# Hashed attention and a squared-ReLU layer on one core: scores and values in 64x64 array tiles taken in turn, hash and totals in 64x32 tiles

## The chip, the cores and the metric

The kernel runs on one core of one Trainium2 chip. The metric is the device time of one execution in microseconds (us). Three runs of the kernel before gave 877.64, 877.53 and 878.19 us; their median is 877.64.

## The reference

Attention over 4 batches of 8 heads, 768 tokens and 64 features, in which a query sees only the keys of its own hash bucket; its output goes through a layer with squared ReLU.

```python
q_bits = np.einsum('bhsd,dk->bhsk', q, proj) > 0        # 6 bits
k_bits = np.einsum('bhsd,dk->bhsk', k, proj) > 0
mask = q_bucket[:, :, :, None] == k_bucket[:, :, None, :]
scores = where(mask, q @ k.T / 8, -1e9)
attn = exp(scores - max); attn = attn / (attn.sum(-1) + 1e-9)
x = (attn @ v) as (4 * 768, 512)
h = np.maximum(x @ w_in, 0)                             # w_in 512 x 2048
out = (h * h) @ w_out                                   # w_out 2048 x 512
```

The weights arrive as 64-bit floats and are rounded to 32 bits on the chip.

## The kernel before

The program has two stages. The first does attention, 16 pairs of heads one after the other; the second, from L717 on, does the layer by a scheme with seven products for eight, and the change leaves its code as it was but for the name of one PSUM pool.

**A pair of heads.** Features stand on the partitions, head 0 on 0 to 63 and head 1 on 64 to 127. `load_pair` (L279) brings q and k through eight DMAs on SP's queue, `features` (L330) turns each by one VectorE transpose. `hash_bits` (L337) multiplies with the projection, in tiles of the array with 64 rows and 32 columns, all eight at once; `signs` (L351) makes bits of it by eight ScalarE operations of 32 partitions, and `weigh` (L379) scales the key bits by one more. Bits are padded into two tiles `bits` on the partitions of the heads.

**Scores.** There are six blocks of 128 keys, `kt`. `score` (L386) makes scores with the keys on the partitions, for the queries 0 to 511 and then 512 to 767 (`CUTS`): for each cut a bf16 product of the bits and an fp32 product of the features into the same PSUM tile, head 0 in rows 0 to 63 of the array and head 1 in rows 64 to 127, with 128 columns each (tiles 64*128, two at once). A PSUM tile `turn` has two banks, one per head; the pool `ps_s` has three of them. ScalarE takes the exponent (L413) into one of four tiles `e`, the ring. An extra column of e holds a tiny constant for the keys that no query meets.

**Totals and values.** `add_up` (L419) adds the six e on VectorE. `attend` (L432) multiplies with the values, 128 keys in the rows and 64 columns per head (tiles 128*64, two at once), over all six blocks into `xo`. `sum_up` (L448) sums `total` over the keys with a matrix of ones (tiles 128*32, four at once), VectorE turns and inverts that, `spread` (L472) multiplies with a selection matrix, and `normalize` (L483) turns the result and multiplies it with xo into `x_t`, which a DMA stores.

**Weights beside it.** Each pair also rounds two pieces of 128x512 weights: `part_weight` (L136, two VectorE operations), `place_power` (L153, two ScalarE operations, L160 and L161), `round_weight` (L163, three VectorE operations). `sum_in` (L522) forms sums of w_in for the second stage.

**Order.** It is written out by hand (`manual_schedule`, the loop from L614); each engine takes its instructions in that order, and SP's DMAs are issued in it. TensorE's order in a pair is: scores of blocks 0 and 1; hash of the next pair; totals of the pair before; values of blocks 4 and 5 of the pair before; `spread`; scores 2 and 3; values 0 and 1; scores 4 and 5; values 2 and 3. `finish` (L579) does the middle of this. After the last pair come its totals, its values 4 and 5 and its `spread`, and right behind that the first product of the second stage (L717). VectorE's order at the end is the sums of blocks 4 and 5, `sum_x` for the second stage, the inversion, two more `sum_x`, `normalize`, and the last piece of weights.

Of the kernel before, what the change touches and what calls it, by code (L numbers as in the profile page):

```python
# [34 lines left out]
def kernel(  # L35
# [25 lines left out]
    CUTS = (0, 512), (512, S)  # L61
# [49 lines left out]
    NIN = 2 * NFT  # L111
    pieces = [
        (moe_w_in, i // 2 * P, i % 2 * HF + j * PIECE) for j in range(2) for i in range(NIN)
    ] + [(moe_w_out, i * P, 0) for i in range(NFF)]
    raws, parts, goals = {}, {}, {}
    ins = [p_t.tile([P, NFT, 2, PIECE], FP32, name=f"in{j}") for j in range(2)]

    def goal(i):
        if i < 2 * NIN:
            return ins[i // NIN][:, i % NIN // 2, i % 2]  # L120
        return p_t.tile([P, DM], FP32, name="out_piece", bufs=3)

    def load_weight(i):
        src, r, c = pieces[i]
        if src.dtype != U64:
            goals[i] = goal(i)
            nc.sync.dma_start(out=goals[i], in_=src[r:r + P, c:c + PIECE])
            return
        raw = p_w.tile([P, PIECE, 2], U32, name="raw", bufs=3)
        nc.sync.dma_start(  # L130
            out=raw.rearrange("p f w -> p (f w)"),
            in_=src.bitcast(U32)[r:r + P, 2 * c:2 * (c + PIECE)],
        )
        raws[i] = raw

    def part_weight(i):  # L136

        if i not in raws:
            return
        high = raws[i][:, :, 1]  # L140
        power = p_w.tile([P, PIECE], U32, name="power")
        top = p_w.tile([P, PIECE], U32, name="top")
        nc.vector.tensor_scalar(
            out=power, in0=high, scalar1=20, scalar2=0x7FF,
            op0=ALU.logical_shift_right, op1=ALU.bitwise_and,
        )
        nc.vector.tensor_scalar(
            out=top, in0=high, scalar1=0xFFFFF, scalar2=0x100000,
            op0=ALU.bitwise_and, op1=ALU.bitwise_or,
        )  # L150
        parts[i] = power, top

    def place_power(i):  # L153


        if i not in parts:
            return
        power = parts[i][0]
        small = p_w.tile([P, PIECE], U8, name="small")
        nc.scalar.activation(out=small, in_=power, func=ACTF.Relu, bias=excess)  # L160
        nc.scalar.activation(out=power, in_=small, func=ACTF.Copy, scale=2.0**23)  # L161

    def round_weight(i):  # L163

        raw = raws.pop(i, None)
        if raw is None:
            return keep_weight(i)
        goals[i] = goal(i)
        low, high = raw[:, :, 0], raw[:, :, 1]
        power, top = parts.pop(i)  # L170
        nc.vector.scalar_tensor_tensor(  # L171
            out=power, in0=high, scalar=0x80000000, in1=power,
            op0=ALU.bitwise_and, op1=ALU.bitwise_or,
        )
        one = top.bitcast(FP32)
        nc.vector.scalar_tensor_tensor(  # L176
            out=one, in0=low, scalar=2.0**-32, in1=top, op0=ALU.mult, op1=ALU.add,
# [7 lines left out]
    def keep_weight(i):  # L185

        t = goals.pop(i)
        j, c = divmod(i, NIN)
        if j >= 2:
            nc.sync.dma_start(out=w_out_1[:, i - 2 * NIN], in_=t)  # L190
        elif c == NIN - 1:
# [31 lines left out]
    picks = const.tile([P, P], FP32, name="picks")  # L223
    which = const.tile([P, 2, HS // 32], FP32, name="which")
    NRING = 4
    ring = [const.tile([P, 2, S + 1], FP32, name=f"e{i}") for i in range(NRING)]
# [4 lines left out]
    def constants():  # L231
# [4 lines left out]
        for h in range(2):  # L236
            r = h * D
            nc.vector.memset(gains[r:r + N + 1], -FAR / 2 * N)
            nc.vector.memset(gains[r:r + N], FAR / 2)
            nc.vector.memset(bases[r:r + N + 1], -FAR / 2 * N)  # L240
            nc.vector.memset(bases[r:r + N], -FAR / 2)
            nc.vector.memset(spans[r:r + N], FAR)
        for r in range(0, P, NR_B):
            nc.vector.memset(lifts[r:r + N + 1], 1.0)
            nc.vector.memset(lifts[r:r + N], -SMALL)
        for pair in all_bits:
# [3 lines left out]
        for e in ring:  # L250
            nc.vector.memset(e[:, :, S:S + 1], TINY)


        for g in range(4):
            cut = picks[:, g * 32:(g + 1) * 32]
            at = 64 * (g // 2)
            nc.gpsimd.tensor_tensor(
                out=cut, in0=ident[:, at:at + 32], in1=ident[:, at + 32:at + 64], op=ALU.add
# [8 lines left out]
    def load_first():  # L267

        for src, name in ((q, "q_nat"), (k, "k_nat")):
            t = p_qk.tile([P, SB, 2, D], FP32, name=name)  # L270
# [4 lines left out]
            nat[0, name] = t  # L275
# [3 lines left out]
    def load_pair(pr):  # L279
# [3 lines left out]
        for src, name in ((q, "q_nat"), (k, "k_nat")):  # L283
            t = p_qk.tile([P, S], FP32, name=name)
            for g in range(4):
                h, e = divmod(g, 2)
                nc.sync.dma_start(  # L287
                    out=t[g * 32:(g + 1) * 32].rearrange("i (c d) -> i c d", d=32),
                    in_=src[b, 2 * j + h].rearrange("(c i) (e d) -> e i c d", i=32, e=2)[e],
                )  # L290
            nat[pr, name] = t
# [10 lines left out]
    def first_features(w, r):  # L302

        if r == 0:
            feat[0, w] = p_f.tile([P, S], FP32, name=f"feat{w}")
        tp = turn("tp")[:, 0]
        for i in range(SB // 2):
# [3 lines left out]
                in_=nat[0, ("q_nat", "k_nat")[w]][:, t].rearrange("p h d -> p (h d)"),  # L311
                identity=ident,
            )
        out = feat[0, w][:, r * HS:(r + 1) * HS]
# [6 lines left out]
    void = ps_o.tile([P, 1024], FP32, name="xo")  # L321

    def keep_busy(n, w=512):

        for _ in range(n):
            nc.tensor.matmul(  # L326
                out=void[:, 0:w], lhsT=busy[:, 0:P], rhs=busy[:, 0:w], start=True, stop=True
            )

    def features(pr, w):  # L330

        feat[pr, w] = p_f.tile([P, S], FP32, name=f"feat{w}")
        nc.vector.transpose(out=feat[pr, w], in_=nat[pr, ("q_nat", "k_nat")[w]])  # L333
# [3 lines left out]
    def hash_bits(pr, banks, ws=(0, 1), cs=(0, 1)):  # L337


        for w in ws:  # L340
            hashed[pr, w] = banks
            for c in cs:
                g = 2 * w + c
                for h in range(2):
# [3 lines left out]
                        rhs=feat[pr, w][rows, c * HS:(c + 1) * HS], start=True, stop=True,  # L348
                    )

    def signs(pr, w):  # L351
        bits[pr, w] = t = all_bits[pr % 2][w]
        for c in range(2):
            at = slice((2 * w + c) * NR_B, (2 * w + c + 1) * NR_B)
            for h in range(2):
                nc.scalar.activation(  # L356
                    out=t[h * D:h * D + NR_B, c * HS:(c + 1) * HS], in_=hashed[pr, w][at, h, 0:HS],
                    func=ACTF.Sign, scale=HUGE, bias=lifts[at],
                )

# [18 lines left out]
    def weigh(pr):  # L379

        t = bits[pr, 1]
        nc.scalar.activation(out=t, in_=t, func=ACTF.Copy, scale=gains)

    weights = {}

    def score(pr, kt):  # L386

        e = ring[len(weights) % NRING]
        weights[pr, kt] = e
        key = slice(kt * P, (kt + 1) * P)  # L390
        sts = []

        def products(st, lo, hi, src, first):
            for h in range(2):
                rows = slice(h * D, (h + 1) * D)
                nc.tensor.matmul(  # L396
                    out=st[:, h, 0:hi - lo], lhsT=src[pr, 1][rows, key],
                    rhs=src[pr, 0][rows, lo:hi], start=first, stop=not first,
                )


        if (pr, kt) == (0, 0):
            for lo, hi in CUTS:
                sts.append(turn("st"))
                products(sts[-1], lo, hi, feat, True)
        for i, (lo, hi) in enumerate(CUTS):
            if len(sts) <= i:
                sts.append(turn("st"))
                products(sts[i], lo, hi, bits, True)
                products(sts[i], lo, hi, feat, False)  # L410
            else:
                products(sts[i], lo, hi, bits, False)
            nc.scalar.activation(  # L413
                out=e[:, :, lo:hi], in_=sts[i][:, :, 0:hi - lo], func=ACTF.Exp, scale=scale
            )

    totals, outs, recs = {}, {}, {}

    def add_up(pr, kt):  # L419

        if kt == 1:
            totals[pr] = p_n.tile([P, 2, S], FP32, name="total")
            nc.vector.scalar_tensor_tensor(
                out=totals[pr], in0=weights[pr, 0][:, :, 0:S], scalar=SB * TINY,
                in1=weights[pr, 1][:, :, 0:S], op0=ALU.add, op1=ALU.add,
            )
        else:
            nc.vector.tensor_tensor(  # L428
# [69 lines left out]

# [984 lines left out]
```

## Time and profile before

| | |
|---|---|
| median of three runs | 877.64 us |
| span of the profiled execution, first to last instruction | 875.8 us |
| attention, first scores to the first product L717 | 9.3 to 330.2 us |
| TensorE busy | 864.5 us (99%) |
| VectorE busy | 760.1 us (87%) |
| ScalarE busy | 391.7 us (45%) |
| GpSimd busy | 107.1 us (12%) |
| mean granted TensorE clock | 0.997 |

The profile gives no time of its own for the profiled execution beyond the span; the median stands 1.8 us above it. A row of instructions names the line, the engine (PE is TensorE, DVE is VectorE, ACT is ScalarE, POOL is GpSimd, SP issues DMAs), the operation, the tiles written and read, and the shape. Behind a TensorE row stands the tile of the array, rows by columns; an fp32 product shows as two passes, so "x4" is two products. A record of a product reaches until its last result has landed, so records of a stream overlap, and its pace is read from the starts.

### The profile page before, as it was taken

The page shows a single profiled execution, that of the slowest core. Times are in us where ns is not written, and L with a number is a line of the kernel's source. Part 1 is how long each engine was busy: PE and PEld are TensorE (multiplying, and loading weights), DVE is VectorE, ACT ScalarE, POOL GpSimd, SP SyncE. Part 2 cuts the span into 40 slices and gives each one's busy share as a digit, 9 for nine tenths or more (in the row PEclk, how much of TensorE's full clock was granted, in tenths as well). Part 3 has the DMA queues.
Part 4 walks back from the last instruction along what each step waited for, and adds up shares of the span by engine and source line. Part 5 has one row for each costly group of instructions (what it writes and reads, how often), then busy time and mean ns, then how long its engine had stood idle before and what let it go on. Part 6 is the DMA issues. An engine that isn't in the chain of part 4 may idle for free.

```text
span 875.8 us, 12135 instructions
## 1 busy us (share of the span) xinstructions
PE 864.5 (99%) x4340; PEld 519.3 (59%) x4340; DVE 760.1 (87%) x1099; ACT 391.7 (45%) x673; POOL 107.1 (12%) x172
## 2 busy tenths in 40 slices
PE   8999999999999999999999999999999999999996
PEld 4444444444444444444688865556888755568885
DVE  5999999999999998888689978888889788888875
ACT  6988788888888852222211123332111233321110
POOL 2000000000000001554032111112000211110002
PEclk9999999999999999999999999999999999999998
DMA  9787967999879526999787874536756754355565
GB/s 176 146 154 134 232 156 150 194 244 234 179 172 226 164 98 223 294 263 288 299 291 259 219 172 156 173 125 219 282 161 177 166 169 152 124 169 158 154 171 109
DMA packets 224131, 167.09 MB, mean 191 GB/s; under 512 B 164448, under 2 KB 181344, under 8 KB 224064
## 3 DMA queue, kind: packets, MB, share of 16 engines
q1 hardware_dynamic: 189152, 87.19, 41.7%
q0 software_dynamic: 12528, 41.30, 15.2%
q10 hardware_dynamic: 22384, 37.76, 14.3%
q8 instruction: 36, 0.59, 0.3%
q14 instruction: 31, 0.25, 0.1%
HBM read 124.52 MB, written 41.68 MB: 190 GB/s over the span
## 4 chain that ended last, share of the span: by engine, by line
PE 95%; DVE 2%; SPq 1%; DMA 1%; issue 0%; ACT 0%; DVEq 0%
PE acc L717 40%; PE st L396 17%; PE acc L936 16%; PE xo L438 13%; PE acc L889 6%; PE hash L346 1%; PE tot L455 1%; DVE total L428 1%; DMA q_nat<-in_q_dram 1%; SPq L287 1%; PE xo L326 0%; PE tp L309 0%; DVE power L171 0%; DVE top L176 0%; DVE feat L333 0%
## 5 line engine op out<-in xcount | busy, mean ns | idle before, releaser
L413 ACT ACTIVATE e<-st 128x1024 f32<-128x1024 f32 x192 | 144.9, 810 | 44.4 <-PE st L396 40.7
L396 PE MATMUL st<-feat,feat 64*128 64x512 f32 (+1 forms) x768 | 150.4, 483 | 0.0
L438 PE MATMUL xo<-e,v_nat 128*64 128x512 f32 (+1 forms) x768 | 134.8, 492 | 0.0
L717 PE MATMUL acc<-b,leaf 128*128 128x256 f32 x600 | 133.1, 379 | 0.0
L717 PEld LDWEIGHTS acc<-b,leaf 128*128 128x128 f32 x600 | 113.8, 190 | 16.2 <-issue 0.9
L428 DVE TENSOR_TENSOR total<-total,e 128x1536 f32<-128x1536 f32 x64 | 112.4, 1756 | 8.1 <-ACT e L413 3.6
L438 PEld LDWEIGHTS xo<-e,v_nat 128*64 128x64 f32 x768 | 51.3, 136 | 82.2 <-issue 74.0
L936 PE MATMUL acc<-t_x,w_unit 128*128 128x512 f32 x192 | 90.2, 592 | 0.0
L396 PEld LDWEIGHTS st<-feat,feat 64*128 64x128 f32 x768 | 66.0, 188 | 32.4 <-issue 22.6
L717 PE MATMUL acc<-t,leaf 128*128 128x256 f32 x336 | 76.2, 380 | 0.0
L356 ACT ACTIVATE bits<-hash,lifts 32x384 bf16<-32x384 f32 x120 | 68.7, 573 | 1.9
L717 PEld LDWEIGHTS acc<-t,leaf 128*128 128x128 f32 x336 | 63.7, 190 | 9.1 <-DVE t L516 0.5
L801 DVE SCALAR_TENSOR_TENSOR b<-h 128x512 f32<-128x512 f32 x96 | 65.7, 692 | 3.0
L396 PE MATMUL st<-bits,bits 64*128 64x256 bf16 (+1 forms) x384 | 63.0, 325 | 0.7 <-ACT bits L356 0.5
L936 PE MATMUL acc<-x,w_unit 128*128 128x512 f32 x128 | 60.1, 592 | 0.0
L717 PE MATMUL acc<-x,w_unit 128*128 128x512 f32 x128 | 56.5, 593 | 0.0
L717 PE MATMUL acc<-b_t,leaf 128*128 128x256 f32 x240 | 53.8, 379 | 0.0
L936 PEld LDWEIGHTS acc<-t_x,w_unit 128*128 128x128 f32 x192 | 36.5, 190 | 28.8 <-issue 26.8
L724 ACT COPY two<-acc 128x256 f32<-128x256 f32 (+1 forms) x29 | 12.5, 432 | 87.7 <-PE acc L717 69.1
L724 ACT COPY one<-acc 128x256 f32<-128x256 f32 (+1 forms) x29 | 12.5, 432 | 84.3 <-PE acc L717 55.5
L717 PEld LDWEIGHTS acc<-b_t,leaf 128*128 128x128 f32 x240 | 45.5, 190 | 6.2
L396 PEld LDWEIGHTS <-bits 64*128 64x128 bf16 x384 | 23.6, 93 | 41.9 <-issue 37.7
(159 smaller groups left out, 1166.5 us busy)
## 6 DMA issues: line engine op xcount, KB each, us to landing
leaf<-w_out ACTq DMA_DIRECT2D x142, 256.0 KB, 3.2
w_unit<-w_in SPq DMA_DIRECT2D x16, 640.0 KB, 4.0
raw<-in_moe_w_in_dram SPq DMA_DIRECT2D x16, 512.0 KB, 5.5
raw<-in_moe_w_out_dram SPq DMA_DIRECT2D x16, 512.0 KB, 4.5
w_unit<-w_in SPq DMA_DIRECT2D x8, 896.0 KB, 7.8
w_out<-sums POOLq DMA_DIRECT2D x16, 448.0 KB, 6.8
sum<-w_in SPq DMA_DIRECT2D x16, 448.0 KB, 4.8
v_nat<-in_v_dram SPq DMA_DIRECT2D x16, 384.0 KB, 4.6
```

Source lines behind the costliest of these rows:

```text
L287: nc.sync.dma_start(out=t[g * 32:(g + 1) * 32].rearrange("i (c d) -> i c d", d=32), in_=src[b, 2 * j + h].rearrange("(c i) (e d) -> e i c ...
L346: nc.tensor.matmul(out=banks[g * NR_B:(g + 1) * NR_B, h, 0:HS], lhsT=projs[rows], rhs=feat[pr, w][rows, c * HS:(c + 1) * HS], start=True, ...
L356: nc.scalar.activation(out=t[h * D:h * D + NR_B, c * HS:(c + 1) * HS], in_=hashed[pr, w][at, h, 0:HS], func=ACTF.Sign, scale=HUGE, bias=li ...
L396: nc.tensor.matmul(out=st[:, h, 0:hi - lo], lhsT=src[pr, 1][rows, key], rhs=src[pr, 0][rows, lo:hi], start=first, stop=not first,)
L413: nc.scalar.activation(out=e[:, :, lo:hi], in_=sts[i][:, :, 0:hi - lo], func=ACTF.Exp, scale=scale)
L428: nc.vector.tensor_tensor(out=totals[pr], in0=totals[pr], in1=weights[pr, kt][:, :, 0:S], op=ALU.add)
L438: nc.tensor.matmul(out=xo[h * D:(h + 1) * D, lo:hi], lhsT=nat[pr, "v_nat"][:, h, kt * D:(kt + 1) * D], rhs=weights[pr, kt][:, h, lo:hi], s ...
L717: nc.tensor.matmul(out=acc[to], lhsT=a(i), rhs=b(i), start=first and i == 0, stop=last and i == n - 1, skip_group_check=True,)
L724: nc.scalar.copy(out=t, in_=acc[of])
L801: nc.vector.scalar_tensor_tensor(out=out, in0=h, scalar=0.0, in1=h, op0=ALU.max, op1=ALU.mult)
L889: nc.tensor.matmul(out=out, lhsT=w[:, a], rhs=b, start=start, stop=stop, skip_group_check=True)
L936: nc.tensor.matmul(out=acc[to], lhsT=w[:, PLACE[a], f], rhs=bt[b](f), start=first and f == 0, stop=last and f == NFT // 2 - 1, skip_group_ ...
```

## The change

**Scores** are made for 64 keys by 64 features by 384 queries: four tiles 64x64 of the array, two heads by two halves of the block of keys. A turn (`score(pr, kt, i)`) covers a block of keys and half of the queries, and ends in an exponent of 128x768. **Values** are made by 64 keys, 64 features of a head and 385 columns, again in four tiles 64x64. The two row halves write into different banks, and swap them in a second turn (`attend(pr, kt, s)`); where the next product would write with the other half of the rows into the bank that the last one wrote, `part` puts a GpSimd memset of one element between the two, so that the second waits for the first through GpSimd. There are four such places in a pair. **Turns** of scores and of values follow each other one by one. **Totals** use tiles 64x32, in two passes before and behind the hash, which has 64x32 as before. **PSUM**: two tiles `turn` where there were three, and one tile `spare` for totals and `spread`. `keep_x` copies xo to SBUF by ScalarE, and `normalize` reads the copy.

**Bits** are made by two ScalarE operations on 128 partitions (sign, then scale) and put in their places by eight DMAs on SP's queue. **Weights** are rounded in double pieces of 128x2x512, one per pair, and VectorE's step that joins sign and power moves from `round_weight` to `part_top`, behind `place_power`. q and k come in one tile and are turned by one transpose. At the end, values 4 and 5 of the last pair go in tiles 128*64 before its totals, and `spread` comes after the inversion with nothing between them on TensorE.

```diff
-    ps_s = first.enter_context(tc.tile_pool(name="ps_s", bufs=3, space=PSUM))
+    ps_t = fast.enter_context(tc.tile_pool(name="ps_t", bufs=1, space=PSUM))
+    ps_s = first.enter_context(tc.tile_pool(name="ps_s", bufs=2, space=PSUM))
...
+    def signs(pr):
+        nc.scalar.activation(
+            out=signed, in_=hashed[pr, 0][:, :, 0:HS], func=ACTF.Sign, scale=HUGE, bias=lifts
+        )
+        nc.scalar.activation(out=signed, in_=signed, func=ACTF.Copy, scale=gains)
+
+    def place_bits(pr):
+        for w in (1, 0):
+            bits[pr, w] = t = all_bits[pr % 2][w]
+            for c in range(2):
+                at = (2 * w + c) * NR_B
+                for h in range(2):
+                    nc.sync.dma_start(
+                        out=t[h * D:h * D + NBITS + 1, c * HS:(c + 1) * HS],
+                        in_=signed[at:at + NBITS + 1, h],
+                    )
...
+    def products(st, i, kt, src, first):
+        cut = slice(i * HS, (i + 1) * HS)
+        for k in range(2):
+            key = slice(kt * P + k * HK, kt * P + (k + 1) * HK)
             for h in range(2):
                 rows = slice(h * D, (h + 1) * D)
                 nc.tensor.matmul(
+                    out=st[k * HK:(k + 1) * HK, h, 0:HS], lhsT=src[1][rows, key],
+                    rhs=src[0][rows, cut], start=first, stop=not first, skip_group_check=True,
+                )
...
+    def part(before, after):
+        step = nc.gpsimd.memset(token, 0.0)
+        tc.add_manual_dep(step.ins, before.ins.name, SYNC)
+        tc.add_manual_dep(after.ins, step.ins.name, SYNC)
...
+    def attend(pr, kt, s):
+        if (kt, s) == (0, 0):
+            outs[pr] = ps_o.tile([P, 2, 512], FP32, name="xo")
+        for r in range(2):
             for h in range(2):
+                done = value(
+                    pr, kt, slice(r * HK, (r + 1) * HK), h, (r + s) % 2,
+                    (kt, s) == (0, 0), (kt, s) == (SB - 1, 1),
+                )
+                if turned.get(pr, s) != s:
+                    part(lasts[pr], done)
+                turned[pr] = s
+        lasts[pr] = done
...
+    def keep_x(pr):
+        raws_x[pr] = p_n.tile([P, 2, HS + 1], FP32, name="x_raw")
+        nc.scalar.copy(out=raws_x[pr], in_=outs.pop(pr)[:, :, 0:HS + 1])
...
+            else:
+                score(pr, 0, 0)
+                attend(old, 4, 0)
+                score(pr, 0, 1)
+                attend(old, 5, 0)
+                add_up(old, SB - 1)
...
+                round_weight(old)
+                if more:
+                    load_weight(pr + 1)
                 for m in sums.get(pr, ()):
                     sum_in(m)
+            score(pr, 1, 0)
+            beside(4, 1)
+            score(pr, 1, 1)
+            beside(5, 1)
...
+                keep_x(old)
+                sum_up(old, 0)
+            if more:
+                hash_bits(pr + 1, turn("hash"))
+                signs(pr + 1)
+                place_bits(pr + 1)
             if pr > 0:
+                if not more:
+                    score(pr, 2, 0)
+                sum_up(old, 1)
+                invert(old)
             add_up(pr, 1)
...
+            part_power(pr)
+            if more:
+                score(pr, 2, 0)
+            attend(pr, 0, 0)
+            score(pr, 2, 1)
+            attend(pr, 1, 0)
+            score(pr, 3, 0)
             if pr > 0:
+                spread(old)
+            attend(pr, 0, 1)
+            score(pr, 3, 1)
+            attend(pr, 1, 1)
+            add_up(pr, 2)
+            if pr > 0:
+                normalize(old)
+                place_power(pr)
+            add_up(pr, 3)
...
+            score(pr, 4, 0)
+            attend(pr, 2, 1)
+            score(pr, 4, 1)
+            attend(pr, 3, 1)
             if pr > 0:
+                part_top(pr)
+            score(pr, 5, 0)
+            attend(pr, 2, 0)
+            score(pr, 5, 1)
+            attend(pr, 3, 0)
             if pr == 0:
                 place_power(0)
             add_up(pr, 4)
+        pr = NP - 1
+        for kt in (SB - 2, SB - 1):
+            attend_whole(pr, kt)
+        keep_x(pr)
         sum_x(0, 1)
+        add_up(pr, SB - 1)
+        for s in range(2):
+            sum_up(pr, s, True)
+        invert(pr)
+        for n in (2, 3):
+            sum_x(0, n)
+        spread(pr)
+        normalize(pr)
         sum_x(0, 4)
+        round_weight(pr)
```

More of the change, by code (lines that the diff above doesn't have):

```diff
@@ L60 @@
     PIECE = 512
[L61 removed]
+    HK = P // 2
     assert (S, D, DM) == (768, 64, 512) and NBITS < D
@@ L150, in part_weight @@
         )
+        nc.vector.scalar_tensor_tensor(
+            out=power, in0=high, scalar=0x80000000, in1=power,
+            op0=ALU.bitwise_and, op1=ALU.bitwise_or,
+        )
         parts[i] = power, top
[L153 to L161, printed above, removed]
     def round_weight(i):
@@ L419, in add_up, with first_score @@
+    def first_score():
+        own = [feat[0][:, w] for w in range(2)]
+        marks = [bits[0, w] for w in range(2)]
+        sts = [turn("st") for _ in range(2)]
+        for i, st in enumerate(sts):
+            products(st, i, 0, own, True)
+        for i, st in enumerate(sts):
+            products(st, i, 0, marks, False)
+            weight(0, 0, i, st)
+    totals, outs, raws_x, spares = {}, {}, {}, {}
+    turned, lasts = {}, {}
     def add_up(pr, kt):
+        e = key_of(pr, kt)[:, :, :, 0:HS]
```

339 lines of the change are left out of this document (155 added, 184 removed).

## The prediction, on record before the changed kernel ran

> **What bounds the kernel now.** I read the page's first two parts, then the chain of waits in order of time, the timeline of TensorE over one pair, and the groups by form. Every sum below is a difference within the profiled execution (span 875.8 us) and is carried over to the median of the runs, 877.64, of which 1.8 lie around the span.
>
> ```profile
> PE 864.5 (99%) x4340; PEld 519.3 (59%) x4340; DVE 760.1 (87%) x1099; ACT 391.7 (45%) x673; POOL 107.1 (12%) x172
> ```
>
> TensorE is busy throughout, and the chain in order of time is nearly all its products:
>
> ```profile
> 48.24 3.34 PE st L396 x24
> ...
> 307.03 3.34 PE st L396 x24
> 311.15 2.74 PE xo L438 x16
> ...
> 327.41 2.74 PE xo L438 x16
> 330.23 181.04 PE acc L717 x616
> ```
>
> The first scores of pair 2 stand at 48.24, those of pair 15 at 307.03: 258.79 / 13 = 19.91 us per pair. The last pair takes 330.23 - 307.03 = 23.2 to the second stage. In 48.24 to 307.03 TensorE is busy 258.8 us, VectorE 249.6 (19.2 a pair, near its limit too), ScalarE 221.9 (17.1). What TensorE loses shows in its timeline (start, length):
>
> ```profile
> 107.90 0.39 PE L396 MATMUL st<-bits,bits 64*128 64x512 bf16 x2
> 108.12 1.02 PE L396 MATMUL st<-feat,feat 64*128 64x512 f32 x4
> 108.98 0.27 PE L396 MATMUL st<-bits,bits 64*128 64x256 bf16 x2
> 109.09 0.60 PE L396 MATMUL st<-feat,feat 64*128 64x256 f32 x4
> 109.53 0.38 PE L396 MATMUL st<-bits,bits 64*128 64x512 bf16 x2
> ...
> 111.24 0.88 PE L346 MATMUL hash<-feat,projs 64*32 64x384 f32 x16
> 112.04 0.85 PE L455 MATMUL tot<-total,ones 128*32 128x384 f32 x8
> 112.82 2.81 PE L438 MATMUL xo<-e,v_nat 128*64 128x512 f32 x16
> 115.46 0.25 PE L477 MATMUL xo<-both,picks 128*64 128x24 f32 x4
> 115.64 0.39 PE L396 MATMUL st<-bits,bits 64*128 64x512 bf16 x2
> ```
>
> By starts, two tiles at once take 0.86 for 512 fp32 columns, 0.43 for 256, 0.22 and 0.11 for bits. All eight tiles of the hash run together: two passes of 384 columns are 0.64 by that pace, and the next start comes after 0.80. So a change of tile shape costs about 0.15. Values: 2 x (0.86 + 0.43) = 2.58, and the next start after 2.64 to 2.74; scores: 3.23 by pace, 3.34. Ideal work in a pair is 3 x 3.23 + 3 x 2.58 + 0.64 + 0.64 = 18.7; the other 1.2 go into some eight changes of shape and `spread` (0.18).
>
> **The change, part by part.**
>
> *Shapes.* The columns streamed stay the same, four tiles at once for two. A turn of scores is 0.16 + 0.64 = 0.81, one of values (385 columns) 0.65; twelve of each 17.45; hash 0.64; totals 4 x 0.16 = 0.65. Scores, values and `spread` now share a shape, so two changes remain (0.30), and `spread` costs 0.1 (below its 0.18, which holds a change). Sum 19.14: 0.77 below 19.91. That alternation inside a shape is free is read from bits and features, which follow at full pace; four 64x64 tiles at once are not in this trace, and the eight of the hash are the nearest row.
>
> *Two PSUM tiles for three.* A turn of scores waits for the exponent two turns earlier. Exponents of 768 columns lie midway between these rows:
>
> ```profile
> L413 ACT ACTIVATE e<-st 128x1024 f32<-128x1024 f32 x96 | 98.6, 1027 | 44.4 <-PE st L396 40.7
> L413 ACT ACTIVATE e<-st 128x512 f32<-128x512 f32 x96 | 57.0, 594 | 0.0
> L160 ACT ACTIVATE small<-power,excess 128x512 uint8<-128x512 uint32 x32 | 22.9, 714 | 0.0
> L161 ACT ACTIVATE power<-small 128x512 uint32<-128x512 uint8 x32 | 20.2, 631 | 1.0
> ```
>
> that is 0.81, against a turn pair of 1.46: ordinarily it fits. But `place_power`, doubled, stands between the exponents of scores (3,1) and (4,0). With the slope of the exponents (0.433 per 512 columns) L160 becomes 1.15, L161 1.06. From the end of scores (3,1): results landed 0.16, to ScalarE 0.05, exponent 0.81, L160 1.15, L161 1.06, exponent (4,0) 0.81, back 0.05 and 0.03 between dependent ones, less 0.2 where independent operations overlap (two exponents at 118.56 take 1.51, not 1.62): 3.92. TensorE reaches scores (5,0), which need that PSUM tile, after three turns of values and two of scores: 3 x 0.646 + 2 x 0.807 = 3.55. So it waits 0.37 in each pair. Bounds: 0 if all of it overlaps, 0.87 if L160 and L161 take twice their rows (1.43, 1.26). I take 0.37, by the slope. Pair: 19.14 + 0.37 = 19.51, a gain of 0.40, times 13 is **-5.2**.
>
> *ScalarE* loses eight signs of 0.57 and a scale of 0.94 and gains a sign of 0.57 + 0.325 = 0.90, a copy like L382 (0.94) and `keep_x`, 0.80 by L724 (0.59 for 512): 14.5 a pair from 17.1. Except for the wait above this is off the path.
>
> *VectorE.* TENSOR_TENSOR takes 0.69 for 512 and 1.76 for 1536 columns, so 0.15 is fixed: five weight operations and one transpose fewer save 0.9, the second half of `both` (0.18) goes back. 18.5 a pair lie inside 19.5. Its order holds: the totals before the hash need the sum of block 5, ready some 2.5 us earlier; `part_top` needs `place_power` and comes just after it. If that cover goes, VectorE becomes the bound at 18.5, which costs nothing yet.
>
> *SP.* Eight more DMAs behind ScalarE's scale, some 0.4 to 0.6 us each to issue like SP's others, landing in 3 to 5: done by 17 of the pair's 19.5, where scores need them. Queued behind are x_t's store, values and q and k of a later pair; SP stood idle 62.5 us before x_t's store (14 waits), which hides 4 us a pair.
>
> *GpSimd's step* (`part`). A turn of scores (0.81) or the hash (0.64) covers the way through GpSimd: landing 0.16, reaction 0.05 (other engines) to 0.30 (GpSimd's DMAs after VectorE), memset 0.11, back 0.05: 0.37 to 0.62. I take nothing; beyond 0.64 each tenth costs 0.1 to 0.4 a pair.
>
> *Start.* The hash of pair 1 waits for the transpose as before (15.6), with one block of scores less behind it. Hash 0.8, eight turns of each kind 11.6: pair 1 begins at 27.9, lasts 19.14 + 2 x 0.37 (the first weights' `place_power` too) and pair 2 begins at 47.8: **-0.4**, to +1 if the doubled first weights hold back the bits' DMAs.
>
> *End.* Before, the inversion of pair 14 began 4.2 us after scores (15,0), now 7.9 after (four turns of each, totals, one turn). From there VectorE is in line: inversion 1.2, four sums 1.8 each, weights 0.69, 0.69 and 1.21, `normalize` 2.0, `sum_x` 1.2, the last sum 1.8, less overlaps: 15.1, so the totals start at 23.0. Behind them 0.7 of totals, 0.2, inversion 1.2, `spread` 0.2, and nothing beside it: L717 starts at 25.4, not 23.2. **+2.2** (1.5 to 2.8). Values 4 and 5, which covered the inversion, are done before it. The second stage is unchanged; its first products do not wait for the last weights.
>
> Sum: -5.2 - 0.4 + 2.2 = -3.4: **874.2 us**; with the bounds of the start and end terms 871 to 877.5.
>
> **A rule that speaks against it.** TENSOR_SCALAR on 512 columns takes 0.42 where two-input forms take 0.69; `part_power` stands where the step of values (0,1) is due. The Trainium skill, "SBUF — State Buffer", section "Who interferes with whom", says that a VectorE instruction in its two-port mode, which tensor_scalar can enter, blocks GpSimd until its end; no row here has both engines at work, so the trace leaves it open.
>
> **The rivals.**
>
> *Behind a VectorE operation (5%).* GpSimd's memset waits for a whole `part_power`, at most 2 x 0.42 = 0.84; the cover has 0.44 left at a 0.05 reaction, so 0.4 a pair, 14 pairs, +5.7: 879.9.
>
> *Slower: GpSimd reacts late (12%).* Its longest row after a wait is 0.78 us. Then a step takes 0.16 + 0.78 + 0.11 + 0.05 = 1.10, 0.29 over a turn of scores at three places and 0.46 over the hash: 1.33 a pair, 15 pairs, +20: 894. It decides from a reaction of 0.3 on. Against it: four memsets in a row start 0.03 apart.
>
> *Slower: ScalarE's block is longer (11%).* At twice the rows, 0.5 more in 14 pairs, +7: 881. For it: both rows hold more than an exponent's.
>
> *No wait at all (15%).* If ScalarE catches up, -0.37 x 14: 869.
>
> *It doesn't do what it says (7%).* Each change between scores and values drains the array as a change of shape does: 24 x 0.13 = 3 us a pair, 920; or four tiles don't run at once, far more. Against both: the hash's eight tiles, and `spread`, which follows values in one shape without a gap.
>
> *Others (8%)*, mostly near no change.
>
> The forecast has 42%. Below 875.9, which is faster by over 0.2% (about what a measurement of this kernel tells from no change), lie 33 of it and "no wait": 48%. Within 0.2% lie 9 of the forecast and 5 of the others: 14%. Slower is the rest, 38%. The range 867.5 to 884 leaves out the late reaction and the failed shapes, two in ten.
>
> **What would show it.** Scores 0.81 and values 0.65 apart by starts; a gap before scores (5,0) that ends with exponent (4,0); 19.5 us from pair to pair; pair 2 near 48, L717 25.4 us after scores (15,0). Wrong: gaps before the values that follow a step, or before the bits' first use in a pair.

## The result, and the profile after

The changed kernel takes 890.76 us (median of 4 runs, 888.8 to 893.17), the kernel before 877.59 beside it: a ratio of 1.0151 (95% interval 1.0138 to 1.0163), 13.2 us slower. The forecast was 874.2, with a range of 867.5 to 884. The profiled execution took 888.8, its span is 886.9: 11.1 more than the 875.8 of before.

```profile
PE 861.4 (97%) x6612; PEld 539.3 (61%) x6612; DVE 751.6 (85%) x1021; ACT 347.2 (39%) x552; POOL 123.6 (14%) x232
```

TensorE is busy 3.1 us less than before (864.5) in a span that is 11.1 longer: what came is waiting. Where it stands is told by the starts of the hash from pair to pair (pair 2's to pair 15's): 19.55, then 19.67 to 19.75 seven times, then 20.95, 20.29, 24.82, 21.97, and 19.67 at last. Before, the first was 20.46 and all others 19.91. Most pairs are shorter by 0.23; four long ones cost 1.27 + 0.61 + 5.14 + 2.29 = 9.3 over 19.68. The chain of waits in order of time (start, us, what) shows the starts of these four pairs; a row `DMA` lasts from the issue of a transfer to its landing:

```profile
206.83 1.77 DMA bits<-signed
...
217.64 7.67 DMA raw<-in_moe_w_out_dram
225.33 3.58 DMA bits<-signed
...
237.83 8.57 DMA raw<-in_moe_w_out_dram
246.41 0.69 SPq L398
...
247.88 5.61 DMA bits<-signed
253.49 0.04 issue
253.53 1.43 PE st L432 x11
254.96 1.28 PE xo L488 x8
256.25 1.43 PE st L432 x12
257.68 0.65 PE xo L488 x8
...
273.89 1.79 DMA bits<-signed
...
341.45 181.05 PE acc L812 x616
```

The scores of a new pair wait for the bits, and in two of the four (20.29 and 24.82) the bits stand in the chain behind the 1 MB of weights ahead of them in SP's queue. L812, the old L717, starts at 341.45, not 330.23; behind it the second stage is as long as before (181.05, 181.04). The timeline of SP for the pair of 24.82 (start, us, engine, line, operation; one row holds several transfers) shows the queue:

```profile
237.83 0.43 SPq L141 DMA_DIRECT2D raw<-in_moe_w_out_dram  x1
238.36 1.35 SPq L219 DMA_DIRECT2D w_in<-s_in  x2
239.82 8.75 SPq L398 DMA_DIRECT2D bits<-signed  x8
...
249.61 8.65 SPq L307 DMA_DIRECT2D qk_nat<-in_q_dram  x4
```

The bits begin 4.6 us after the hash (235.24) and take 8.75. Five are issued by 244.2; the sixth starts at 246.41, the moment the weights have landed (237.83 + 8.57). In four of the nine pairs without loss they begin 2.87 after the hash and take 6.1 to 6.6; in the other five they begin 3.8 to 6.3 after it. Then four loads of q hold SP for 8.65 us (in a pair without trouble, from 110 to 118 us, one took 0.5 to 2). By the waits of SP from 50 to 300 us (us in all, times, longest), it stood 52.6 us in front of x_t's store (L497) before; now (L591) 1.6: where it had time in hand, it is behind.

```profile
SPq L497 <- DVE power L143: 52.6, 12, 10.8
```

In the pairs of 20.29 and 24.82 the issue alone is not what makes the bits late. In the pair of 24.82 the last two bits transfers were issued 11.9 and 12.6 us after the hash (247.15 and 247.88). In a pair that lost nothing (hash at 95.49) they were issued later, 12.3 and 13.1 after it (107.81 and 108.55). But here the last took 5.61 us to land, where the transfers of 206.83 and 273.89 took 1.77 and 1.79: a load of 2 MB of x (GpSimd's queue, from 246.36) and the long loads of q move at the same time. In the pair of 20.29 the transfer of 225.33, issued 10.4 us after the hash, took 3.58. The pairs of 20.95 and 21.97 are late by their issue: their bits begin 8.05 and 8.26 us after the hash.

### The profile page after: what moved, and what is told of

Read it like the earlier page. It is cut to its first block, busy times and chain, and to the rows that moved or that the text cites. A ratio compares the mean times of both kernels' runs of the same rounds, so it can differ in the third digit from the quotient of the medians.

```text
span 886.9 us, 16832 instructions
## 1 busy us (share of the span) xinstructions
PE 861.4 (97%) x6612; PEld 539.3 (61%) x6612; DVE 751.6 (85%) x1021; ACT 347.2 (39%) x552; POOL 123.6 (14%) x232
## 3 DMA queue, kind: packets, MB, share of 16 engines
q10 hardware_dynamic: 22384, 37.76, 13.9%
## 4 chain that ended last, share of the span: by engine, by line
PE 84%; DMA 5%; ACT 5%; DVE 2%; SPq 2%; issue 1%; ACTq 0%; DVEq 0%
PE acc L812 39%; PE acc L1031 15%; PE st L432 12%; PE xo L488 8%; PE acc L984 5%; ACT e L438 2%; DMA raw<-in_moe_w_out_dram 2%; DMA bits<-signed 2%; ACT power L165 1%; PE tot L537 1%; ACT small L164 1%; SPq L307 1%; PE hash L367 1%; SPq L398 1%; DMA v_nat<-in_v_dram 1%; DVE total L475 1%
## 5 line engine op out<-in xcount | busy, mean ns | idle before, releaser
L438 ACT ACTIVATE e<-st 128x768 f32<-128x768 f32 x192 | 153.6, 809 | 94.7 <-PE st L432 83.7
L432 PE MATMUL st<-feat 64*64 64x384 f32 x1536 | 163.0, 485 | 1.0 <-DVE feat L336 1.0
L488 PE MATMUL xo<-e,v_nat 64*64 64x385 f32 (+1 forms) x1520 | 163.3, 487 | 0.5 <-DMA v_nat<-in_v_dram 0.5
L812 PE MATMUL acc<-b,leaf 128*128 128x256 f32 x600 | 133.0, 379 | 0.0
L812 PEld LDWEIGHTS acc<-b,leaf 128*128 128x128 f32 x600 | 113.9, 190 | 16.0 <-issue 0.6
L488 PEld LDWEIGHTS xo<-e,v_nat 64*64 64x64 f32 (+1 forms) x1520 | 63.8, 133 | 56.0 <-issue 43.9
L432 PE MATMUL st<-bits,bits 64*64 64x384 bf16 x768 | 70.7, 328 | 9.3 <-DMA bits<-signed 6.3
L432 PEld LDWEIGHTS st<-feat 64*64 64x64 f32 x1536 | 61.7, 133 | 29.7 <-issue 25.1
L812 PE MATMUL acc<-t,leaf 128*128 128x256 f32 x336 | 76.3, 380 | 0.0
L812 PEld LDWEIGHTS acc<-t,leaf 128*128 128x128 f32 x336 | 63.6, 190 | 9.3 <-DVE t L602 0.5
L432 PEld LDWEIGHTS <-bits 64*64 64x64 bf16 x768 | 29.5, 107 | 52.7 <-issue 46.5
L483 POOL MEMSET token<- 1x1 f32 x62 | 16.6, 269 | 309.1 <-PE xo L488 258.6
L812 PE MATMUL acc<-x,w_unit 128*128 128x512 f32 x128 | 56.5, 593 | 0.0
L812 PE MATMUL acc<-b_t,leaf 128*128 128x256 f32 x240 | 53.8, 379 | 0.0
L812 PEld LDWEIGHTS acc<-b_t,leaf 128*128 128x128 f32 x240 | 45.5, 190 | 6.2
```

Of the source, the lines that this page charges most:

```text
L432: nc.tensor.matmul(out=st[k * HK:(k + 1) * HK, h, 0:HS], lhsT=src[1][rows, key], rhs=src[0][rows, cut], start=first, stop=not first, skip_ ...
L438: nc.scalar.activation(out=key_of(pr, kt)[:, :, i, 0:HS], in_=st[:, :, 0:HS], func=ACTF.Exp, scale=scale)
L483: step = nc.gpsimd.memset(token, 0.0)
L488: return nc.tensor.matmul(out=outs[pr][h * D:(h + 1) * D, c, 0:HS + 1], lhsT=nat[pr, "v_nat"][rows, h, kt * D:(kt + 1) * D], rhs=key_of(pr ...
L812: nc.tensor.matmul(out=acc[to], lhsT=a(i), rhs=b(i), start=first and i == 0, stop=last and i == n - 1, skip_group_check=True,)
```

## The experiments

The theory after the first look: **queue order**. The bits are late because they stand behind the 1 MB load in SP's one queue. Rivals: too many bytes for the DMA engines whatever the queue; SP's time itself; GpSimd's steps.

### The load moved behind the bits

```
 round_weight(old)
-if more: load_weight(pr + 1)
...
 place_bits(pr + 1)
+if pr > 0: load_weight(pr + 1)
```

> The change with one step moved: the load of the next double weight piece (1 MB) is issued behind the eight bits transfers of its pair, not ahead of them. Theory (queue order: the bits' transfers stand in SP's queue behind that load, move only after its bytes, and the sixth is issued only when it has landed): the long pairs (20.95, 20.29, 24.82, 21.97) go back to 19.68, which takes 9.3 off 890.8: 881.5, and no TensorE gap before scores names bits any more. Rival (too many bytes in these pairs, whatever the order): within 1.5 of 890.8. Rival (lateness only moves on to the loads of values, queries and keys behind it): 884 to 890, with gaps that name v_nat or feat.

912.09 us, ratio to before 1.0389 (1.0364 to 1.0414): 21 worse than the change, and above every expectation. The theory as I had put it falls; lateness moves on, as the last rival said, but costs far more than its 884 to 890. The first pairs are as they were; from the hash of pair 5 on they are 20.5 to 25.7, and gaps name bits and v_nat. SP's timeline around a load:

```profile
112.88 0.62 SPq L141 DMA_DIRECT2D raw<-in_moe_w_in_dram  x1
113.60 0.54 SPq L591 DMA_DIRECT2D x_all<-x_t  x1
114.24 0.37 SPq L316 DMA_DIRECT2D v_nat<-in_v_dram  x1
114.66 7.89 SPq L307 DMA_DIRECT2D qk_nat<-in_q_dram  x4
```

The loads of q right behind the weights now hold SP for 7.89 us, waiting for no semaphore. They are not urgent, but the stores and the next pair's bits are queued behind them: in these pairs bits begin 7.2 to 12.2 us after the hash, not 2.87. This points to SP's time in order, not to who stands ahead of the bits in one pair.

### The same, with place_power parted

```
 small = Relu(power - 896)                 # behind the exponent of (3,1), as before
-power = small * 2**23
 score(pr, 4, 0)
+power = small * 2**23
```

> As the run with the load behind the bits, and the two operations of place_power are parted: the Relu stays behind the exponent of scores (3,1), the Copy stands behind that of scores (4,0). Theory (the 0.37 us by which the turn before scores (5,0) is long in pairs 1 to 15 is ScalarE's block of 2.2 us between two exponents): 15 x 0.37 = 5.5 off, 876.0; pairs of 19.31. Rival (VectorE, busy some 18.6 of 19.7 us a pair, is the next bound, or the later Copy makes part_top and the sums behind it late): 879 to 882, the gap moves to products that wait for VectorE.

913.69, ratio 1.0399 (1.0384 to 1.0414). Pairs that no transfer disturbs take 19.34 to 19.43 for 19.67, and the gap before scores (5,0) is gone: the wait on ScalarE is what the prediction said it was. The time does not fall at all, and neither expectation had that: what TensorE no longer waits for ScalarE it waits for SP.

### The bits the old way

```
-signed = Sign(hash); signed = signed * gains; eight transfers
+eight Sign operations, each from the hash into its place in bits
 ...
+weigh(pr + 1)                             # ahead of scores (5,0)
```

> The change with its bits edit undone: eight Sign operations of ScalarE write the bits in place and a scale follows late in the pair, no transfers. Theory: the bits' lateness (9.3) is gone, but eight signs (4.6 us) hold one of only two PSUM turn tiles and ScalarE; TensorE reaches scores (2,1), which need that tile, 1.8 us after the hash, so it waits some 3 us a pair: 881.5 + 14 x 3 = 923. Rival (the signs fit beside the turns as they did with three tiles): 881 to 884.

949.02, ratio 1.0805 (1.0768 to 1.0841), 26 above the 923 expected. Every pair waits 2.93 us for the signs, as expected; three pairs are 22.85, near the 22.7 expected, and ten are 24.2 to 25.8, because the turns after that wait run at half pace (below). With two PSUM tiles for turns, the old way is no choice: the transfers are part of the price of the shapes.

### The kernel before with the bits edit alone

```
-signs(pr + 1, 1); signs(pr + 1, 0); ... weigh(pr + 1)
+signs(pr + 1); place_bits(pr + 1)         # two operations, eight transfers
```

> The kernel before with the bits edit alone: two operations of ScalarE and eight transfers per pair; scores, values, totals and 512 KB weight loads as before. Theory (the transfers are harmless behind loads of 512 KB, which landed in some 5 us, and ScalarE's relief of 2.6 us a pair is off the path): 877.6, within 1.5. Rival (eight transfers at 0.69 us to issue are late by themselves): 885 or more, gaps before scores that name bits in most pairs.

883.82, ratio 1.0072 (1.0058 to 1.0086). Between the two expectations: from the third on all pairs are 19.91 but one of 23.88. There two loads of k held SP 4.17 and 4.11 us beside the 2 MB load of x (the bits' issue took 6.07 as ever). So eight transfers fit into SP's slack behind 512 KB loads, but such a stall, which cost nothing before (there two loads of q took 3.27 and 3.10 at that place), now delays something urgent.

### The load by GpSimd

```
-load_weight(pr + 1)                       # nc.sync, behind round_weight
 ...
 invert(old)
+load_weight(pr + 1, nc.gpsimd)
```

> The change with the loads of double weight pieces 2 to 15 issued by GpSimd, behind the step of the totals, in place of SP. Theory, as it stands after the run that only moved that load behind the bits (912.09): SP issues everything in order and stalls on the loads of q and k when 1 MB stands ahead of them, so whatever is behind, the bits first, is late; what counts is that SP's own queue is free. Then the long pairs go back to 19.68: 881.5, at most one of them (pair 12, with 2 MB of x) still long by up to 4, 885.5. Rival (the DMA engines are full of bytes in these pairs, whichever queue they come from): 888 to 892, bits late as before. Rival (GpSimd's issue of a load, 0.91 us in the x load's row, makes its steps late): 19.68 becomes 20 and more, gaps that name the token.

888.84, ratio 1.0128 (1.0113 to 1.0143): 1.9 of the 11 us, the first rival's time. The pairs that were 20.29 and 24.82 are 19.68 and 19.67; but the first of the four is 21.16, its bits begun 9.1 us after the hash, and the one behind x's load is 25.95. In that one SP was held 5.58, 3.42 and 4.79 us by single loads of q and k, the bits began 13.9 after the hash, and values and bits were late. So SP is late also where the 1 MB is not in its queue.

### The same, with three edits more

```
 parted place_power; and
-sum_x(0, 1); add_up(15, 5)
+add_up(15, 5); sum_x(0, 1)
-first_keys(1, ...); ... features(1)
+features(1); first_keys(1, ...)
```

> As the run with the loads by GpSimd, and three edits more: place_power parted around the exponent of scores (4,0); in the last pair the sum of block 5 ahead of the first sum_x; in pair 0 the transpose of pair 1's q and k ahead of the second half of the first keys. Theory: off the time of that run 0.33 x 14 = 4.6 for the first (the split run's pairs of 19.34 to 19.36 without lateness, against 19.67), 1.0 for the second (the gap before the last totals) and 1.7 for the third (the gap before the hash of pair 1): 7.3 less, 874.2 if that run gives 881.5, below the kernel before. Rival (VectorE or the transfers take the place of what goes): less than 4 off.

889.2, ratio 1.0149 (1.0135 to 1.0164): nothing off, as the rival said. Steady pairs are 19.35, but others 21.8, 21.4 and 24.45: SP needs its time, and a faster TensorE only waits more.

### The load in halves

```
 load_weight(pr + 1, half 0)               # 512 KB where the 1 MB stood
 ...
 load_values(pr + 1)
+load_weight(pr + 1, half 1)
```

> The change with each double weight piece still one tile and one set of operations, but loaded by two transfers of 512 KB in SP's queue: the first where the load of 1 MB stood, the second behind the load of the values, as the loads of single pieces stood before the change. Theory (1 MB in one piece ahead of the bits is what holds SP and the bits; b1_before_bits_moved, with 512 KB, had one long pair of 23.88 only): lateness falls from 9.3 to some 4 to 5, 886. Rival (the second half now holds SP on the loads of q and k, as the whole piece did behind the bits): 895 to 912.

896.38, ratio 1.0225 (1.021 to 1.024). The rival is right: the second half stands right ahead of the loads of q and k, and pairs of 24.16 and 24.94 come of it. The size of one load is not the cause.

### Two edits of order

```
 the last two edits above, on the change itself
```

> The change with two edits of order alone: in the last pair the sum of block 5 ahead of the first sum_x; in pair 0 the transpose of pair 1's q and k ahead of the second half of the first keys. Theory (the misses of the end, 1.0, and of the start, 1.7 of 2.0, are VectorE's order and nothing else): 2.7 off, 888.1. Rival (what is gained at the start is given back, since SP's transfers of the bits of pairs 1 and 2 are then late): 889.5 to 891.

886.19, ratio 1.0132 (1.0093 to 1.0171), scattered from 883.42 to 896.61. In the profile pair 2's hash is at 34.84, 1.74 earlier; the gap before the last totals (1.02) is gone, and from scores (15,0) to the second stage it is 24.8 for 25.7: both come from VectorE's order, and together they give 2.6 of the 2.7 expected. The rest of the difference is the long pairs, which differ from run to run; one of 26.4 stays.

### The bits by GpSimd

```
-nc.sync.dma_start(out=bits..., in_=signed...)      # eight, behind signs
 invert(old)
+nc.gpsimd.dma_start(...)                           # two
 ...
 attend(pr, 0, 1)
+nc.gpsimd.dma_start(...)                           # six
```

> The change with the eight bits transfers issued by GpSimd, in place of SP: two behind the step of the totals, six behind the step of values (0,1). The load of 1 MB and all else stay on SP. Theory (SP's one queue, in order, is what makes the bits late: it stalls on bulk loads while the DMA engines are full; the bits themselves are 5 KB each and need little of the engines): no gap before scores names bits from pair 2 on, pairs of 19.68, 881.5; up to 3 more if the values of pairs 13 and 14 are late behind the loads of x and units: 881 to 885. Rival (the DMA engines are full of bytes, so that 5 KB wait in any queue): 888 or more, bits late in pairs 10 to 13. Rival (GpSimd's issues, 0.55 to 0.75 each by its other loads, run into its steps before values (0,1) and (2,0)): 20 or more per pair, gaps that end with the token.

879.69, ratio 1.0023 (1.0013 to 1.0034): 11.1 less than the change, with the same bytes, the same transfers and the 1 MB load where it was. All pairs are 19.55 to 19.75, and no gap before scores names bits after pair 1. GpSimd's timeline in a pair:

```profile
118.11 1.03 POOL L397 DMA_DIRECT2D bits<-signed  x2 [2.65 <-ACT signed L389]
119.36 0.60 POOL L482 MEMSET token<- 1x1 f32 x1 [0.21 <-PE xo L487]
119.83 3.08 POOL L397 DMA_DIRECT2D bits<-signed  x6
125.42 0.43 POOL L482 MEMSET token<- 1x1 f32 x1 [2.50 <-PE xo L487]
131.62 0.09 POOL L482 MEMSET token<- 1x1 f32 x1 [5.77 <-PE xo L487]
```

Eight bits take 4.1 us of GpSimd, 0.51 each, always 3.13 after the hash. The engines stay as full as before (80.5% in SP's queue between 100 and 300 us), and a bits transfer still takes 1.5 to 7.4 us to land. But all eight are issued by 7.9 us after the hash, where SP issued the last 11.9 to 15.3 after it in the four long pairs: full engines do not make 5 KB late that are issued in time. The edit moves the bits to another issuer and to another queue at once; which of the two counts for more is not shown. The Trainium skill, "DMA: Bandwidth & Descriptors", section "Issuing engines are not separate DMA queues", says that all issuers share the same 16 engines and that spreading transfers only saves the time to initiate them, usually small. The first half agrees with the landings of up to 7.4 us beside SP's loads; but here that time, with SP's stalls in it, is 6.1 to 8.75 us a pair for the bits alone, and moving it is worth 11 us.

### Long rows for q and k

```
-in_=src[...].rearrange("(c i) (e d) -> e i c d", i=32, e=2)[e]     # rows of 128 bytes
+in_=src[...].rearrange("(e i c) d -> e i (c d)", i=32, e=2)[e]     # rows of 3072 bytes
```

> The change with q and k loaded in rows of 3072 bytes in place of 128 (the same eight transfers of 96 KB per pair, the same queue and order); the elements then stand in other places than the transpose needs, so the scores are those of other numbers. Theory (SP's stalls come from the loads of q and k, whose 6144 packets of 128 bytes took some 17 ns each, 6.7 us of all 16 DMA engines per pair, and fill the queue): SP never stalls long, bits on time, 881.5, at most one late pair (885). Rival (1 MB of weights ahead of the bits is the whole cause): pairs 9 to 12 long as before, 888 or more.

884.72, ratio 1.0086 (1.0071 to 1.0101): 6.0 less than the change, at the upper end of what the theory allowed. Its profiled execution is the fastest of four; its span, 878.7, is 8.2 below the change's, with one pair of 20.64 and one of 20.16. The load of 1 MB stands ahead of the bits as in the change. The queue's row between 100 and 300 us (packets, MB, share of 16 engines), of the change and then of this run:

```profile
q1 hardware_dynamic: 87294, 35.16, 79.1%
```

```profile
q1 hardware_dynamic: 36811, 37.83, 66.8%
```

The packets go from 87,294 to 36,811 and the engines' share by 12 points, with no fewer bytes, and the longest issue of a load of q or k between 50 and 300 us takes 1.90 in place of 4.07: packets of 128 bytes fill the engines, and SP stalls on the loads that make them.

### Bits by GpSimd and the three edits

```
 the bits by GpSimd, place_power parted, the last sum and pair 1's transpose first
```

> As the run with the bits by GpSimd, and the three edits of e6_gpsimd_split_tail_start (place_power parted, the last sum ahead of sum_x, pair 1's transpose first). Theory: 4.6 + 1.0 + 1.7 = 7.3 less than e9_bits_by_gpsimd; 874.2 if that gives 881.5, faster than the kernel before by 0.4%. Rival (values late behind bulk loads, or VectorE, busy some 18.6 of 19.3 us, take it back): 877 to 884.

874.14 us, ratio 0.9951 (0.9938 to 0.9965): faster than the kernel before by 0.5%. Most pairs are 19.35 (two are 19.71 and 19.74); 5.5 us off e9_bits_by_gpsimd, not 7.3. By the profiles the pairs give 3.6 of the 4.6, the start 1.4 of the 1.7, and the end 0.42 of the 1.0: the gap before the last totals shrinks from 1.03 to 0.55, that before `spread` stays (1.24). Besides, in this profile the first products of the second stage run at a granted clock of 0.50 (325.02 to 328.43), which costs 1.5. That the time meets the 874.2 expected is chance: e9_bits_by_gpsimd came out 1.8 lower, and the three edits gave 1.8 less. With SP relieved, the edits count that were worth nothing beside a late SP.

### Longer steps of GpSimd

```
 step = nc.gpsimd.memset(token, 0.0)
+for _ in range(4):
+    step = nc.gpsimd.memset(token, 0.0)
```

> The run with the bits by GpSimd (879.69), and five memsets in place of one in each of GpSimd's steps, each behind the one before. Four more at 0.09 and some 0.05 between them make a step 0.56 longer (an estimate from the memsets of 0.09 and the 0.05 in which engines react). Theory (the steps are covered by one turn of scores, but two of the four in a pair only just: before values (0,1) and (2,0) the memset takes 0.60 and 0.43 beside a tensor_scalar of VectorE and ends some 0.05 before TensorE needs it): those two lose 0.5 each, the other two, 0.5 and 0.35 shorter, next to nothing: 1.0 to 1.2 a pair, 15 us in 14 pairs, 895. Rival (half a us and more of cover at every step): 880 to 882. Rival (the memset of 0.60 is only recorded so, the step itself ends earlier): all four alike, 880 or 903 and more.

899.66, ratio 1.0249 (1.0232 to 1.0266), between the theory's 895 and the second rival's 903; pairs of 21.07, 1.39 more, for steps that are 0.59 longer. TensorE's timeline in a pair:

```profile
122.67 0.56 PE L538 MATMUL tot<-total,ones 64*32 64x192 f32 x16 [0.28 <-POOL token L485]
...
126.90 0.25 PE L572 MATMUL tot<-both,picks 64*64 64x24 f32 x4
127.67 0.88 PE L489 MATMUL xo<-e,v_nat 64*64 64x385 f32 x8 [0.52 <-POOL token L485]
```

By starts, values (0,1) come 0.58 later, the second totals 0.48, values (4,1) 0.27, values (2,0) not at all. So the step is covered, with nothing to spare at (0,1), 0.1 at the totals, 0.3 at (4,1); at (2,0), where I expected none, the wait on ScalarE beside it covers the whole step.

## Why the prediction was wrong, point by point

**The failed step is "SP".** It said: "Eight more DMAs behind ScalarE's scale, some 0.4 to 0.6 us each to issue like SP's others, landing in 3 to 5: done by 17 of the pair's 19.5", and that SP's idle time "hides 4 us a pair". The size was off: a bits transfer takes 0.69 to issue, eight take 6.1 with their gaps, more than those 4; and the landing took 5.61 in the worst pair. And the step took idle time on a queue for cover that can be drawn on at any moment. SP issues in order; when the engines are full, a load of q or k takes 3 to 6 us to issue. Before, the wait for x_t lay in the queue anyway, and all that stood behind a stall was needed a pair later. The bits are the first item there with a deadline: the pair's first scores start 13.4 us after the hash (115.21, 128.59), the second turn 1.5 later. Shown by e9_bits_by_gpsimd: the one edit of who issues them takes 11.1 us off; e10_long_rows shows what makes SP stall. What the bits cost on SP is 9.3 by the spans of the profiled runs.

What a theory of mine missed after that: I read the 1 MB load out of the chain as the cause. It is what the chain ends on, but when it was moved (e1_load_behind_bits), halved (e7_raw_in_halves) or given to GpSimd (e5_raw_by_gpsimd), lateness came elsewhere. A chain names the last wait, not the resource that is short. How often exactly which load stalls is left open: it differs from run to run.

**Shapes: right, 0.2 short.** Scores are 0.81 apart and values 0.65, hash 0.64, with no drain between scores and values. By starts a pair has 0.17 that I did not count: `spread` takes 0.19, not 0.10, values (0,1) 0.70, not 0.65, and some 0.02 lie around the totals.

**The wait on ScalarE: right.** Values (3,1) to scores (5,0):

```profile
124.66 0.83 PE L488 MATMUL xo<-e,v_nat 64*64 64x385 f32 x8
125.68 0.36 PE L432 MATMUL st<-bits,bits 64*64 64x384 bf16 x4 [0.20 <-ACT e L438]
```

1.02 in place of 0.65, the 0.37 of the sum. Parting place_power gives 0.33 of it back. So a pair is 19.68 for 19.51, a gain of 0.23, not 0.40: 2.2 us over 13 pairs.

**The start: 2.0 late,** by VectorE's order. `first_keys` of the second half waits for its hash, which now comes behind both halves of the first scores, and the transpose for pair 1 queues behind it: pair 2 starts at 49.84, not 47.8.

**The end: right, 0.3 late.** It took 25.7 from scores (15,0) at 315.68 to L812 at 341.38, not 25.4 (23.2 before). The gap before the last totals, where `sum_x` stands ahead of the last sum, was in the prediction's line of VectorE.

Without SP's step the sum would still have been off. In e9_bits_by_gpsimd the pairs are 2.3 above it, the start 1.8 and the end 0.3, and the second stage, which it took as unchanged, is 0.8 longer (546.5 for 545.6). These make 5.2, and its span is just that far off: 1.8 above before, where the sum said 3.4 below. So even with SP's step as forecast the kernel would have come out near 879.4, slower and not faster: every term that was off was off to the same side. (The bounds of the start and the end give 873.5 to 876.2; the 871 to 877.5 beside the forecast does not come out of them.)

**GpSimd's step: right, with less room than I said.** No value of the change waits for a step by more than 0.05, so the rival of 894 did not come. The memset is 0.09 alone and 0.60 or 0.43 when VectorE's `part_power` or `part_top` runs: it ends when that operation ends. The rule of the Trainium skill that the prediction weighed ("SBUF — State Buffer", "Who interferes with whom") agrees with this: GpSimd is blocked to the end of such an operation. So the mechanism of the 5% rival was there. But its price, 0.4 a pair, did not come: `part_power` takes 0.69, not 0.84, and the block ends just when TensorE needs the token (119.96 by the timeline of e9_bits_by_gpsimd, where values (0,1) start at 120.02).

## What to carry to other kernels

Count a DMA queue as an engine with a queue of its own: its issue time, its order, and how long one issue lasts when the DMA engines are full. Idle time there is cover only for what may be late; before a transfer with a deadline goes into a queue of bulk loads, give it a queue that has none, and issue it early enough to land among those loads. And where a chain ends on a transfer, move the late one to another queue before you rearrange what stands ahead of it.

## What the runs showed of the hardware

*A wait of TensorE costs more than itself.* In the pair of 24.82 the wait was 2.60 + 0.32, and the three turns after it took 1.43, 1.28 and 1.43 for 0.81, 0.65 and 0.81: 1.9 us more. By stretches (us from the start, length, busy times, granted clock, DMA share, GB/s):

```profile
253.50:255.00 1.50, 1.47 (x15) 1.24 (x18) 1.50 (x2) 0.00 (x0) 0.00 (x0) 0.66 1.02 415
255.00:256.30 1.30, 1.30 (x14) 0.93 (x10) 0.80 (x2) 0.81 (x1) 0.00 (x0) 0.50 1.12 326
...
257.70:260.00 2.30, 2.30 (x44) 1.47 (x44) 0.00 (x0) 1.63 (x3) 0.00 (x0) 1.00 1.21 138
```

The granted clock falls to 0.50 and is back at 1.00 by 257.7. A wait of 1.43 (275.07) was followed by no such turns. Those of 2.93 in e3_bits_the_old_way were in ten pairs; in the three of 22.85 they were not (granted clock 1.00 behind the wait that ended at 93.92). The records of the clock in that run's trace tell them apart: half rate comes in stretches of 3.41 or 6.83 us, and each begins a whole number of 3.41 us behind the first pair's, at 45.15. In the 3.41 us before that one TensorE was busy for 0.78. The wait that ended at 93.92 is cut by the boundary at 92.93, with 1.47 of work in the 3.41 us before it and 2.43 in those behind it. The stretches behind that wait and behind one that ended at 141.30:

```profile
93.90:95.40 1.50, 1.48 (x21) 0.84 (x24) 0.00 (x0) 1.16 (x2) 0.00 (x0) 1.00 0.00 0
```

```profile
141.30:142.80 1.50, 1.50 (x12) 0.81 (x15) 0.00 (x0) 0.79 (x1) 0.00 (x0) 0.50 0.00 0
```

In the traces of all these runs, from 20 us on, half rate followed every such stretch of 3.41 us in which TensorE stood for 2.0 us or more, and began after none with less than 1.3; between the two it sometimes did. The Trainium skill, "TensorE: Matmul & The Clock Gate", "Part 1: The HAM clock gate", tells of half rate after an idle window of about 3.4 us that runs freely; these boundaries agree with a window that runs by itself, but 2.0 us of idleness in it were enough here.

*SP's transfers in flight.* The sixth bits transfer, the eighth issue behind the load of weights with the stores between, began when that load landed, with SP idle for 2.2 us before. In the trace it signals on the same semaphore as that load, one of eight that SP's transfers take in turn. By the waits of SP (raw to L398, 6.4 us in five) it happens in other pairs too.

*Issue times.* A transfer of 7 rows of 768 bytes takes 0.69 us of SP and 0.51 of GpSimd.
